# A routed expert stage: where the weight conversions of each expert stand

## The chip, the cores and the metric

One core of one Trainium2 chip runs the whole kernel. The metric is the device time of an execution in microseconds; the kernel before took 772.2 us (median of three runs). TensorE is called PE in the rows, ScalarE ACT, VectorE DVE, GpSimd POOL and SyncE SP.

## What is computed

Three stages follow each other. The first is attention over 4 batches, 8 heads, 512 local and 32 global positions with a band of 32. The second mixes each position with the one before it and runs a feed-forward block with a squared Relu and a gate. The third, which the change is about, sends each of 2176 positions to one of 8 experts:

```
logits = x @ w_gate                       # 8 experts
e      = argmax(logits) or the previous position's e, by a local gate
h      = max(x @ w1[e], 0)                # 512 -> 1024
out    = p[e] * (h @ w2[e])               # 1024 -> 512
```

With this input the experts 0 to 7 get 242, 127, 267, 483, 495, 321, 218 and 23 positions.

## The kernel before, in words

The matmuls work in pairs of parts: each float32 operand is split into a high part (rounded) and a low part (the rest), and `mm3` (L19) issues three matmuls for one product: high by high, high by low, low by high.

The weights of an expert are 4 MB, in 8 pieces of 512 KB: four of w1, then four of w2. A piece is fetched from memory by SP into one of five staging buffers (`st`, `sw`; `part`, L768) and then converted (`split`, L772): ScalarE writes the high part into a slot (L779) and VectorE, or GpSimd for the fourth and the eighth piece (`PP`, L35), subtracts it for the low part (L782). `whole` (L790) does that for the next piece in line, gives its staging buffer back and issues the next fetch (`fetch`, L764). Expert e converts the 8 pieces of expert e+1; the slots are double, one set for even and one for odd experts. Each engine runs its instructions in the order in which the program issues them (`manual_schedule`, L1081), so the place of a `whole()` call in the code is its place in the queues of ScalarE, VectorE, GpSimd and SP.

Experts 0 and 1 have one static tile of 128 rows each (`one`, L941). It calls `tall` (L899): the rows stand still and w1 streams, in two halves of 512 columns. Each half ends in a Relu on ScalarE (L918), then four transposes (`turn`, L902) bring it to the layout of the second product, with a copy on ScalarE (L906) and a subtraction on VectorE (L907). The first half's `turn` comes after two of the four steps of the second half's matmuls; the second half's stands after step 2 of the second product (`TW[2]`, L944). `tall` takes five conversions and places three ahead of the first half, one behind its Relu and one behind the first `turn` (`TW`, L909 to L919). The other three stand after steps 3, 5 and 7 of the second product (L946). Between these stand the preparations of the next expert's rows (`X`): four transposes, a copy on ScalarE and a subtraction on VectorE.

Experts 2 to 6 (`expert`, L961) have a count that is known only at run time (`c`, in units of 32 rows), so their code is a nest of branches. The case with 384 rows or more (`big`) stands first in the code, then 352, 320, 288 and 256 rows (`joined`), then one tile (`single`), then none (`none`). A wide case calls `wide` (L887): w1 stands still and the rows stream in 8 steps of 12 matmuls, each followed by a Relu on ScalarE (L894) and a subtraction on VectorE (L895); there are four PSUM buffers for the steps. Conversions stand behind steps 2, 4 and 6 (`FW`, counted from 0), preparations behind 3, 5 and 7 (`FX`). Then `out_` and `product` do the second product for each tile of rows, 24 matmuls each, and `place` scales the result on VectorE and scatters it from GpSimd.

Of the 8 conversions of an expert, five stand in its side of the branch. The last tile's product (L999) stands behind the join, once for all sides, and holds the other three, after its steps 2, 4 and 6, as well as the preparation of the next expert's third tile (`third`). With the counts above, expert 2 runs the side for 288 rows, 3 and 4 the widest, 5 that for 352 and 6 that for 256. Expert 7 (23 rows) runs `one` again, without conversions.

Of the kernel before, what the change touches and what calls it, by code (L numbers as in the profile page):

```python
# [13 lines left out]
P=128; D=512; F=1024; E=8; SG=32; SL=512; S=544; NB=4; T=2176; HD=64; NK=9; NCH=17  # L14
# [4 lines left out]
def mm3(nc,out,wh,wl,xh,xl,first,last,order=None):  # L19

    i=nc.tensor.matmul(out,wh,xh,start=first,stop=False)  # L21
    if order: order(i)
    nc.tensor.matmul(out,wh,xl,start=False,stop=False)  # L23
    return nc.tensor.matmul(out,wl,xh,start=False,stop=last)  # L24
# [7 lines left out]
GA=6; PA=6  # L32
ND=[k for k,n in enumerate([1, 5, 5, 11, 3, 4, 6, 16]) for _ in range(n)]
V7=[1,1,2,2,3,3,3,3]
PP=(0,0,0,1,0,0,0,1); TW=(1,1,1,(2,4,6),3)  # L35
NR=4; NP=4
FX=(3,5,7); WJ=(288,320,352); MW=352; FW=(2,4,6); NW=(2,3); NST=2
def tiles(n): return 4*n-3
LAT=0.2; DLAT=2.1; SLACK=dict(P=0.15,A=0,D=0,G=0)
def op(e,d,need=(),free=(),when=None): return e,d,need,free,when  # L40
# [1 line left out]
class Sched:  # L42
# [11 lines left out]
    def one(s):  # L54

        for x in sorted(s.L,key=lambda x:(s.t<x[3]+(SLACK.get(x[2][0],0) if x[4] else 0),x[0])):
            e,d,need,free,when=x[2]
            if x[3]>s.t or (e and s.busy[e]>s.t) or any(s.places[k]<need.count(k) for k in need) or (when and not when()): continue
            for k in need: s.places[k]-=1
            if e:  # L60
                end=s.t+d; s.busy[e]=end; later=end+(DLAT if e in "QW" else LAT)
                s.left+=[(later,k) for k in free]
            s.next(x)
            if e: same=x[2] and x[2][0]==e; x[3]=end if same else later; x[4]=not same
            return True
# [686 lines left out]
class Experts:  # L752
# [19 lines left out]
    def split(s,e,which,q,st,pool=False):  # L772
# [4 lines left out]
        else:  # L777
            yield "A",.95
            nc.scalar.activation(h[:,qs],st,AF.Copy)  # L779
        if not pool: pool=PP[4*which+q]  # L780
        yield ("G",2.46) if pool else ("D",1.14)
# [76 lines left out]
    def rows(s,i,n=256): return [t[:,:,i[1]:i[1]+n] for t in s.x[i[0]]]  # L858
# [28 lines left out]
    def wide(s,i,e,N,W=(),X=()):  # L887

        nc=s.nc; W=list(W); X=list(X); w1h,w1l=s.views(e,0); xh,xl=s.rows(i,N); hh,hl=[t[:,:,:N] for t in s.h]
        for f in range(8):  # L890
# [4 lines left out]
            nc.vector.scalar_tensor_tensor(out=hl[:,f],in0=ph,scalar=0.0,in1=hh[:,f].bitcast(F32),op0=ALU.max,op1=ALU.subtract)  # L895
            if f in FX: s.go(X)
            if f in FW: s.go(W)
        s.go(X,8); s.go(W,8)
    def tall(s,i,e,W=(),X=None):  # L899

        nc=s.nc; W=list(W); w1h,w1l=s.views(e,0); xh,xl=s.rows(i); hh,hl=s.h
        def turn(b):  # L902
            pt=s.ps.tile([P,4,P],F32,tag="ph",name="pht2",bufs=4)
            for f in range(4): nc.tensor.transpose(pt[:,f],hs[b][:,f*P:(f+1)*P],s.ident)
            sl=slice(4*b,4*b+4)
            nc.scalar.activation(hh[:,sl,:P],pt,AF.Copy)  # L906
            nc.vector.tensor_sub(hl[:,sl,:P],pt,hh[:,sl,:P].bitcast(F32))  # L907
        hs=[]
        s.go(W,TW[4])  # L909
        for b in range(2):  # L910
            ph=s.ps.tile([P,512],F32,tag="ph",name="pht",bufs=4)
            bs=slice(b*512,(b+1)*512)
            for d in range(4):
                if b and d==2:
                    turn(0); s.go(W,TW[1])
                mm3(nc,ph,xh[:,d,:P],xl[:,d,:P],w1h[:,d,bs],w1l[:,d,bs],d==0,d==3)
            hs.append(s.work.tile([P,512],F32,tag="osb",name="hs",bufs=2))
            nc.scalar.activation(hs[b],ph,AF.Relu)  # L918
            if b==0: s.go(W,TW[0])  # L919
        if X is None: return lambda: turn(1)  # L920
        for f in X: f()
        s.go(W,8); turn(1)
# [18 lines left out]
    def one(s,i,e,b,W,X,o=None):  # L941

        W=list(W); last=s.tall(i,e,[W.pop(0) for _ in range(min(5,len(W)))])
        g=dict((f,[]) for f in range(8)); g[TW[2]].append(last)  # L944
        for f,x in zip((0,3,4),X): g[f].insert(0,x)
        for f,w in zip(TW[3],W): g[f].append(w)  # L946
        s.product(b,e,slice(0,P),g); s.place(b,*s.cols(e,0),o=o)
    def more(s,i,e,k,c,d=0):

# [10 lines left out]
            with two.Else(): single()  # L960
    def expert(s,i,i2,e,c,rows,own,X,third):  # L961

        tc=s.tc; keep=s.loaded,list(s.staged),list(s.free); W=[s.whole]*5
        def begin(k=0,early=True):
            s.loaded,s.staged,s.free=keep[0],list(keep[1]),list(keep[2])
            ch=e*NCH+s.o[e]+2*k
            s.nc.gpsimd.tensor_copy(s.at,s.idx[:,ch:ch+2]); s.nc.gpsimd.tensor_copy(s.by,s.pcol[:,ch:ch+2])
            if early: rows()
        def second(W): s.product(1,e,slice(P,2*P),dict(zip((0,2),([w] for w in W))))
        def big():  # L970
            begin(1,False)
            s.wide(i,e,256,W[:3],[own,lambda: (rows(),X[0]()),X[1]])
            s.out_(0,e,0,slice(0,P),{2:W[:1]}); s.out_(1,e,1,slice(P,2*P),{2:W[:1]})
            with tc.If(c>=tiles(4)) as four:
                s.wide(i2,e,256); second([])
            with four.Else(): s.tall(i2,e,[],[])
        def joined(N):
            begin()
            s.wide(i,e,N,W[:3],X)
            if N>256: s.out_(0,e,2,slice(256,N))  # L980
            second(W[:2])
        def single():
            begin(); s.tall(i,e,W,X)
        def none():
            begin()
            for g in (*W,*X): g()
        L=WJ
        def chain(k):
            if k==len(L): big(); return
            with tc.If(c>=tiles(3)+k+1) as up: chain(k+1)  # L990
            with up.Else(): joined(L[k])
        with tc.If(c>=tiles(2)) as two:
            with tc.If(c>=tiles(3)) as up: chain(0)
            with up.Else(): joined(256)
        with two.Else():
            with tc.If(c>=1) as some: single()
            with some.Else(): none()
        s.place(1,s.by[:,1:2],s.at[:,1:2])
        s.product(0,e,slice(0,P),{1:[third],2:[s.whole],4:[s.whole],6:[s.whole]})  # L999
        s.place(0,s.by[:,0:1],s.at[:,0:1])  # L1000
    def run(s):
        tc=s.tc; K=s.K
# [103 lines left out]
```

## Time and profile before

| | us |
|---|---|
| three runs | 768.14, 772.20, 773.02 |
| median | 772.2 |
| the profiled execution | 773.22 |
| its span, first to last instruction | 771.5 |
| mean granted TensorE clock in it | 0.973 of full speed |

The profiled execution is one more run, with the hardware profiler on; its rows are read below. Its span is 1.7 us shorter than its time, which is what lies before the first and behind the last instruction. The first two stages end near 536 us; expert 0's and 1's tiles run from there to 566, experts 2 to 6 to 754, expert 7 to the end.

### The profile page before, as it was taken

The page shows a single profiled execution, that of the slowest core. Times are in us where ns is not written, and L with a number is a line of the kernel's source. Part 1 is how long each engine was busy: PE and PEld are TensorE (multiplying, and loading weights), DVE is VectorE, ACT ScalarE, POOL GpSimd, SP SyncE. Part 2 cuts the span into 40 slices and gives each one's busy share as a digit, 9 for nine tenths or more (in the row PEclk, how much of TensorE's full clock was granted, in tenths as well). Part 3 has the DMA queues.
Part 4 walks back from the last instruction along what each step waited for, and adds up shares of the span by engine and source line. Part 5 has one row for each costly group of instructions (what it writes and reads, how often), then busy time and mean ns, then how long its engine had stood idle before and what let it go on. Part 6 is the DMA issues. An engine that isn't in the chain of part 4 may idle for free. (4 is left out here: it accounts for less than half of the span.)

```text
span 771.5 us, 13972 instructions
## 1 busy us (share of the span) xinstructions
PE 726.4 (94%) x4702; PEld 611.4 (79%) x4702; DVE 496.9 (64%) x1477; ACT 389.9 (51%) x974; POOL 345.0 (45%) x480
## 2 busy tenths in 40 slices
PE   5888888999999999999999899999989999999997
PEld 3555676889898888898888789777777998889795
DVE  6698878968578587587675693577754624435361
ACT  4787566665265565464664442243643613334251
POOL 5566858644626346437245251211643422404421
PEclk9997799999999999999999999999999999999999
DMA  6585133121210321211110320042884633606530
GB/s 150 134 239 147 58 77 107 42 66 23 65 43 3 79 53 24 73 37 40 42 24 14 123 83 28 19 146 65 314 292 137 240 120 109 205 30 193 165 129 24
DMA packets 93185, 76.37 MB, mean 99 GB/s; under 512 B 70350, under 2 KB 74446, under 8 KB 93074
## 3 DMA queue, kind: packets, MB, share of 16 engines
q1 hardware_dynamic: 89618, 64.27, 28.0%
q0 software_dynamic: 3456, 10.75, 4.1%
q8 instruction: 53, 0.87, 0.5%
q14 instruction: 58, 0.48, 0.2%
HBM read 66.08 MB, written 9.44 MB: 98 GB/s over the span
## 5 line engine op out<-in xcount | busy, mean ns | idle before, releaser
L223 POOL TENSOR_SCALAR pl<-pl,mx 128x192 f32<-128x192 f32 (+1 forms) x128 | 64.0, 512 | 86.1 <-DVE mx L220 40.5
L217 ACT ACTIVATE pl<-pl,mx 128x224 f32<-128x224 f32 (+1 forms) x128 | 58.8, 461 | 34.8 <-DVE mx L214 28.0
L21 PE MATMUL psk<-xs,slot0h 128*128 128x256 f32 x256 | 74.6, 297 | 0.8 <-ACT xs L447 0.8
L23 PE MATMUL psk<-xs,slot0h 128*128 128x256 f32 x256 | 73.6, 289 | 0.0
L24 PE MATMUL psk<-xs,slot0l 128*128 128x256 f32 x256 | 73.4, 288 | 0.0
L449 POOL TENSOR_TENSOR xs<-xm,xs 128x512 fp32r<-128x512 f32 (+1 forms) x36 | 46.7, 1309 | 40.2 <-ACT xs L447 40.2
L894 ACT ACTIVATE hh<-ph 128x256 fp32r<-128x256 f32 (+2 forms) x56 | 22.4, 400 | 76.3 <-PE ph L24 45.9
L442 POOL TENSOR_SCALAR xm<-xT,mut 128x256 f32<-128x256 f32 (+7 forms) x96 | 42.7, 461 | 36.8 <-DVE xT L293 17.9
L21 PE MATMUL psv<-slot1h,kh 128*128 128x512 f32 x136 | 55.3, 406 | 0.0
L23 PE MATMUL psv<-slot1l,kh 128*128 128x512 f32 x136 | 54.3, 400 | 0.0
L24 PE MATMUL psv<-slot1h,kl 128*128 128x512 f32 x136 | 54.2, 398 | 0.0
L895 DVE SCALAR_TENSOR_TENSOR hl<-ph,hh 128x256 fp32r<-128x256 f32 (+2 forms) x56 | 24.7, 442 | 44.2 <-ACT hh L894 42.2
L229 PE MATMUL ptp<-ident,pl 128*128 128x128 f32 x256 | 44.1, 292 | 6.8 <-DVE qT L120 1.3
L21 PEld LDWEIGHTS psk<-xs,slot0h 128*128 128x128 f32 x256 | 48.9, 194 | 1.8 <-ACT xs L447 0.9
L23 PEld LDWEIGHTS psk<-xs,slot0h 128*128 128x128 f32 x256 | 48.9, 191 | 1.2
L24 PEld LDWEIGHTS psk<-xs,slot0l 128*128 128x128 f32 x256 | 48.9, 191 | 0.6
L237 PE MATMUL av<-ph,v 128*128 128x256 f32 x192 | 44.7, 293 | 2.2 <-DVE xT L293 1.8
L866 POOL DMA_INDIRECT xs<-y,idx x23 | 24.8, 1078 | 46.9 <-PE pt L873 22.4
L445 DVE SCALAR_TENSOR_TENSOR xm<-xT,mut,xm 128x256 f32<-128x256 f32 (+7 forms) x96 | 41.4, 464 | 3.2 <-POOL xm L442 3.0
L120 DVE TENSOR_TENSOR plo<-ptp,ph 128x512 fp32r<-128x512 f32 x48 | 32.7, 685 | 14.9 <-ACT ph L118 14.7
L21 PE MATMUL ph<-xh,slot2h 128*128 128x256 f32 (+1 forms) x128 | 37.9, 296 | 4.2 <-issue 4.2
L229 PEld LDWEIGHTS ptp<-ident,pl 128*128 128x128 f32 x256 | 30.6, 148 | 13.8 <-issue 3.3
(740 smaller groups left out, 2396.5 us busy)
## 6 DMA issues: line engine op xcount, KB each, us to landing
st<-in_moe_w_dram SPq DMA_DIRECT2D x42, 512.0 KB
sw<-in_moe_w_dram SPq DMA_DIRECT2D x22, 512.0 KB
y<-r SPq DMA_DIRECT2D x17, 256.0 KB
qn<-in_q_l_dram SPq DMA_DIRECT2D x32, 128.0 KB
kn<-in_k_l_dram SPq DMA_DIRECT2D x32, 128.0 KB
earlyh<-in_moe_w_k_dram SPq DMA_DIRECT2D x8, 512.0 KB
raw<-in_moe_w_v_dram SPq DMA_DIRECT2D x8, 512.0 KB
vn<-in_v_l_dram SPq DMA_DIRECT2D x24, 96.0 KB
```

The source lines that it names most:

```text
L21: i=nc.tensor.matmul(out,wh,xh,start=first,stop=False)
L23: nc.tensor.matmul(out,wh,xl,start=False,stop=False)
L24: return nc.tensor.matmul(out,wl,xh,start=False,stop=last)
L120: nc.vector.tensor_sub(out[1],x,out[0].bitcast(F32))
L217: nc.scalar.activation(p[:,h,ks],p[:,h,ks],AF.Exp,bias=mx[:,h:h+1],scale=-1.0,accum_out=mx[:,4+h:5+h])
L223: nc.gpsimd.tensor_scalar(out=p[:,h,ks],in0=p[:,h,ks],scalar1=mx[:,6+h:7+h],scalar2=0.0,op0=ALU.mult,op1=ALU.add)
L229: nc.tensor.transpose(pt[:,c,h],p[:,h,c*96:c*96+P],s.ident)
L237: nc.tensor.matmul(o,s.v(u,x,i,c),P_[y][:,c],start=c==m==0,stop=c==1 and m==len(parts)-1)
L442: nc.gpsimd.tensor_scalar(out=x[:,u,o:o+k],in0=s.xT[b][:,c,q:q+k],scalar1=m[:,1,c:c+1],scalar2=0.0,op0=ALU.mult,op1=ALU.add)
L445: nc.vector.scalar_tensor_tensor(out=x[:,u,o:o+k],in0=s.xT[b][:,c,1+q:1+q+k],scalar=m[:,0,c:c+1],in1=x[:,u,o:o+k],op0=ALU.mult,op1=ALU.add)
L449: nc.gpsimd.tensor_sub(xl[:,cs,:n],x[:,:,:n],xh[:,cs,:n].bitcast(F32))
L866: s.nc.gpsimd.indirect_dma_start(out=s.xs[i][:,j,:],out_offset=None,in_=s.y,in_offset=IndirectOffsetOnAxis(ap=s.idx[:,ch:ch+1],axis=0))
```

## The change

`TW` becomes a pair: its first entry, for expert 0, holds the old numbers, its second, for the experts from 1 on, puts one conversion ahead of the first half, one behind its Relu, two behind the first `turn` and one behind the second half's Relu. In experts 2 to 6 the three conversions leave the product behind the join; each side of the branch gets eight in its place, with `FW` longer and conversions added to the earlier products.

```diff
-PP=(0,0,0,1,0,0,0,1); TW=(1,1,1,(2,4,6),3)
+PP=(0,0,0,1,0,0,0,1); TW=((3,1,1,0),(1,1,2,1)); TF=(2,4,6)
-FX=(3,5,7); WJ=(288,320,352); MW=352; FW=(2,4,6); NW=(2,3); NST=2
+FX=(3,5,7); WJ=(288,320,352); MW=352; FW=(1,2,4,6,7); NST=2
...
         hs=[]
-        s.go(W,TW[4])
+        n=TW[e>0]
+        s.go(W,n[0])
         for b in range(2):
...
                 if b and d==2:
-                    turn(0); s.go(W,TW[1])
+                    turn(0); s.go(W,n[2])
...
             nc.scalar.activation(hs[b],ph,AF.Relu)
-            if b==0: s.go(W,TW[0])
+            s.go(W,n[1+2*b])
...
-        g=dict((f,[]) for f in range(8)); g[TW[2]].append(last)
+        g=dict((f,[]) for f in range(8)); g[1].append(last)
...
-        for f,w in zip(TW[3],W): g[f].append(w)
+        for f,w in zip(TF,W): g[f].append(w)
...
-        tc=s.tc; keep=s.loaded,list(s.staged),list(s.free); W=[s.whole]*5
+        tc=s.tc; keep=s.loaded,list(s.staged),list(s.free); W=[s.whole]*8
...
-        def second(W): s.product(1,e,slice(P,2*P),dict(zip((0,2),([w] for w in W))))
+        def second(W): s.product(1,e,slice(P,2*P),{0:W[:1],1:W[1:2],2:W[2:]})
...
-            s.out_(0,e,0,slice(0,P),{2:W[:1]}); s.out_(1,e,1,slice(P,2*P),{2:W[:1]})
+            s.out_(0,e,0,slice(0,P),{0:W[:1],2:W[:1],4:W[:1]}); s.out_(1,e,1,slice(P,2*P),{0:W[:1],2:W[:1]})
...
-            s.wide(i,e,N,W[:3],X)
-            if N>256: s.out_(0,e,2,slice(256,N))
-            second(W[:2])
+            s.wide(i,e,N,W[:5 if N==256 else 4],X)
+            if N>256: s.out_(0,e,2,slice(256,N),{0:W[:1],2:W[:1],4:W[:1]})
+            second(W[:3 if N==256 else 1])
...
-        s.product(0,e,slice(0,P),{1:[third],2:[s.whole],4:[s.whole],6:[s.whole]})
+        s.product(0,e,slice(0,P),{1:[third]})
```

The sides `single` and `none` pass `W` on as it is, so they too get eight in place of five.

## Rows read from the trace of the kernel before

**Rows 1.** The page, part 1: busy time, share of the span, instructions.

```profile
PE 726.4 (94%) x4702; PEld 611.4 (79%) x4702; DVE 496.9 (64%) x1477; ACT 389.9 (51%) x974; POOL 345.0 (45%) x480
```

**Rows 2.** Busy time by stretch: expert 1, expert 3 (columns in the first line).

```profile
core 0: us, PE busy (x) PEld busy (x) DVE busy (x) ACT busy (x) POOL busy (x), PEclk, DMA share, GB/s
...
549.90:566.20 16.30, 13.93 (x69) 10.56 (x67) 12.82 (x13) 10.77 (x15) 12.06 (x8) 1.00 0.91 326
...
601.30:648.20 46.90, 46.90 (x305) 42.60 (x305) 19.02 (x31) 16.13 (x28) 14.29 (x13) 1.00 0.40 135
```

**Rows 3.** Waits of TensorE, 535 to 772: us in total, times, longest us.

```profile
PE ph L21 <- issue: 4.5, 3, 2.8
PE pht L904 <- ACT slot2h L779: 1.8, 1, 1.8
PE pht L904 <- ACT hs L918: 0.5, 1, 0.5
```

**Rows 4.** Timeline of ScalarE, expert 1: start us, us, what, [idle before <-releaser].

```profile
549.48 2.22 ACT L779 ACTIVATE slot2h<-sw 128x1024 fp32r<-128x1024 f32 x2
554.38 1.06 ACT L779 ACTIVATE slot2h<-st 128x1024 fp32r<-128x1024 f32 x1 [2.68 <-DMA st<-in_moe_w_dram]
555.34 0.58 ACT L918 ACTIVATE hs<-pht 128x512 f32<-128x512 f32 x1
556.09 1.06 ACT L779 ACTIVATE slot2h<-st 128x1024 fp32r<-128x1024 f32 x1 [0.16 <-DMA st<-in_moe_w_dram]
...
558.98 1.06 ACT L779 ACTIVATE slot0h<-st 128x1024 fp32r<-128x1024 f32 x1 [1.35 <-DMA st<-in_moe_w_dram]
559.95 0.58 ACT L918 ACTIVATE hs<-pht 128x512 f32<-128x512 f32 x1
```

**Rows 5.** Timeline of TensorE, expert 1.

```profile
552.39 0.39 PE L24 MATMUL pht<-slot1h,xl 128*128 128x512 f32 x1
...
555.98 0.65 PE L904 MATMUL pht<-ident,hs 128*128 128x128 f32 x4 [1.84 <-ACT slot2h L779]
...
560.58 0.66 PE L904 MATMUL pht<-ident,hs 128*128 128x128 f32 x4 [0.54 <-ACT hs L918]
...
563.39 0.39 PE L24 MATMUL po<-slot3h,hl 128*128 128x512 f32 x1
```

**Rows 6.** Timeline of VectorE, expert 1.

```profile
560.08 1.23 DVE L782 TENSOR_TENSOR slot0l<-st,slot0h 128x1024 fp32r<-128x1024 f32 x1 [1.72 <-ACT slot0h L779]
561.22 0.68 DVE L876 TENSOR_TENSOR xl<-pt,xh 128x512 fp32r<-128x512 f32 x1
561.90 0.69 DVE L907 TENSOR_TENSOR hl<-pht,hh 128x512 fp32r<-128x512 f32 x1
```

**Rows 7.** Timeline of TensorE: the first matmuls of experts 2, 5 and 6.

```profile
569.08 0.58 PE L21 MATMUL ph<-xh,slot2h 128*128 128x288 f32 x1 [2.77 <-issue]
...
695.74 0.40 PE L21 MATMUL ph<-xh,slot1h 128*128 128x352 f32 x1 [0.35 <-issue]
...
730.77 0.39 PE L21 MATMUL ph<-xh,slot2h 128*128 128x256 f32 x1 [1.41 <-issue]
```

**Rows 8.** Busy time by stretch: ahead of these three, and behind the first.

```profile
564.00:566.20 2.20, 2.20 (x11) 1.56 (x9) 1.74 (x4) 1.81 (x3) 1.87 (x2) 1.00 1.05 420
693.00:695.20 2.20, 2.20 (x11) 1.59 (x9) 2.18 (x2) 1.69 (x2) 0.43 (x1) 1.00 0.11 13
727.00:729.20 2.20, 2.20 (x11) 1.55 (x9) 2.16 (x2) 1.66 (x2) 0.46 (x1) 1.00 0.88 313
...
569.10:572.40 3.30, 3.30 (x14) 3.30 (x15) 0.00 (x0) 0.00 (x0) 2.69 (x6) 0.52 0.89 281
```

**Rows 9.** Timeline of SP's queue, expert 5's end: fetches of weights.

```profile
722.99 2.18 SPq L770 DMA_DIRECT2D sw<-in_moe_w_dram  x2
728.05 3.72 SPq L770 DMA_DIRECT2D st<-in_moe_w_dram  x3
```

**Rows 10.** Timeline of ScalarE, expert 6: the Relu behind step 2.

```profile
735.35 0.39 ACT L894 ACTIVATE hh<-ph 128x256 fp32r<-128x256 f32 x1 [1.03 <-PE ph L24]
```

## The prediction

> **What bounds the kernel now.** I read the page first: TensorE is busy for 94% of the span [rows 1]. A sum over the whole span says little about the part that the diff touches, so I took busy time by stretch next. The reader is to see that in the stretch of expert 3 TensorE is busy for every microsecond, while ScalarE has 16.13 of 46.90, and that only the stretch of expert 1 shows a real hole, 13.93 busy of 16.30 [rows 2]. Then the waits of TensorE alone in the expert stage: three lines carry nearly all of it, 4.5 us in three pieces with no releaser, and 1.8 and 0.5 us behind ScalarE in expert 1 [rows 3]. So the stage is bound by matmuls, and an edit that moves ScalarE, VectorE and GpSimd work can win at most those 6.8 us and what a stall does to the clock. I then looked at each hole by itself.
>
> The two holes of expert 1: the transposes of the first half start at 555.98 after 1.84 us of idle, those of the second half at 560.58 after 0.54 [rows 5]. ScalarE's order explains both. The Relu of the first half starts at 555.34, right behind the third of three conversions, and that one began only at 554.38, when its piece of weights landed; the Relu of the second half (559.95) stands behind the fifth, which began at 558.98, again on a landing [rows 4].
>
> The three pieces without a releaser are the first matmuls of experts 2, 5 and 6 (2.77, 0.35 and 1.41 us) [rows 7]. Those are the experts that leave the nest of branches by an Else; experts 3 and 4, which fall through to the widest case, show no hole. I read them as jumps. In the 2.2 us ahead of them the DMA engines were 1.05, 0.11 and 0.88 busy [rows 8], in the same order as the holes. After the longest hole TensorE's granted clock was 0.52 for the next 3.30 us, its lower level of 1.2 GHz [rows 8]; at full clock that work is 3.30 x 0.52 = 1.7 us, so the hole of expert 2 costs 2.77 + 1.6 = 4.4 us in all.
>
> **The change, part by part.** Number the conversions of an expert 1 to 8. With this input experts 2 to 6 have 267, 483, 495, 321 and 218 rows, so they run the cases 288, widest, widest, 352 and 256. The number of conversions executed stays the same; only their places change.
>
> *Expert 1: the order 3, 1, 1, 0 becomes 1, 1, 2, 1.* Conversion 1 runs at 549.48 as now, about 1.06 us [rows 4]. The first half's last matmul ends at 552.39 + 0.39 = 552.8 [rows 5]; the Relu (0.58) follows at once and ends near 553.4. TensorE has six more matmuls before it needs that, until 554.1, so the 1.84 us hole goes. The transposes end near 554.5, the copy of the first half (0.58) near 555.1, with conversion 2 ahead of it in the gap. Conversions 3 and 4 have data by 554.38 and 556.09 [rows 4]; they run 555.1 to 557.2 and the second Relu to 557.8. TensorE meanwhile does the rest of the second half to about 555.9, and then the first two steps of the product (0.70 each) with four transposes (0.36) between, to about 557.7; up to 0.3 us more if VectorE's low part comes late behind conversion 2. So the second hole nearly goes as well, and the transposes of the second half end near 558.4. Next late is conversion 5. In ScalarE's order it still stands ahead of the second half's copy, and its data land at 558.98 whatever ScalarE did before in expert 1: with five staging buffers it refills the one that expert 0's last conversion gave back. It ends at 560.0, one copy of activations (0.6) follows, and the second half's copy ends at 561.1. On VectorE conversion 5's subtraction (560.08), the activations' (561.22) and then the second half's low part (561.90 for 0.69) keep the times that they have now [rows 6]. Step 4 of the product needs this low part in its third matmul: earliest 562.6, against 563.39 in the trace [rows 5]. What follows is unchanged work, so expert 1 ends 0.8 us earlier: 2.38 us of holes go and 1.6 come back at step 4. Bounds: 2.4 us if conversion 5 lands early enough for everything; the other end is a loss of 0.5, if conversion 2, now 3 us later, lets its staging buffer go late and the refill lands late in turn. I take 0.8, the row of VectorE's low part.
>
> *Experts 2 to 6: conversions out of the last product.* They run beside 24 matmuls that are all back to back (2.20 busy of 2.20 while ScalarE has 1.66) [rows 8], so removing them there frees no time on TensorE by itself. Behind them on VectorE and GpSimd only the last scaling and scatter move up, and nobody on TensorE waits for those.
>
> *The same conversions earlier, after steps 1, 2, 4, 6, 7 of the wide half, and in the earlier products.* In the 256 case ScalarE stands idle for 1.03 us ahead of a Relu [rows 10] and a conversion takes 1.05: it fits to within some hundredths, and four PSUM buffers stand between a late Relu and TensorE. I take 0; without that cover it is under 0.1 us for each added conversion, five experts, so 0.5 us at most. All five staging buffers are full when an expert begins, conversions 6 to 8 need refills that are asked for after 1 to 3, more than 5 us earlier. The fetches that SP issues and GpSimd's two subtractions (conversions 4 and 8) move up with them; in GpSimd's queue conversion 4 still stands behind all gathers that the expert issues, so it delays none of them, and in front of a scatter at most, whose end only GpSimd's next copies wait for.
>
> *Transfers ahead of the jumps.* This is the part that I expect to reach TensorE. SP issues fetches at 722.99 and again at 728.05 [rows 9], because conversions 6 to 8 of expert 5 sit in its last product; they keep the DMA engines at 0.88 just before the jump into expert 6. In the changed kernel the last of them is issued near 723 and lands before 729, so the jump meets quiet DMA engines, like the jump into expert 5 now: 1.41 - 0.35 = 1.06 us less. Bounds: 0 and 1.41. Expert 5's jump has quiet engines already. Expert 2's doesn't change: expert 1 keeps its three conversions in the product, and the fetches behind them still fill the engines.
>
> Sum against the profiled execution: 773.22 - 0.8 - 1.06 = 771.4. That execution lies 1.0 above the median of the runs, 772.2, so as a median I forecast 770.4.
>
> **A rule of the skill that speaks against this.** The Trainium skill, "Runtime: NRT & Kernel Launch", section "Instruction fetch mechanics", says that prefetch is purely sequential and that a taken branch to a target outside of the two fetched pages has to wait for the page. It does not tie the wait to other traffic. By that rule, the trace agrees so far, since only the taken jumps show holes [rows 7]; whether the load or the target's place sets their length, three jumps can't say. By the place alone the sum would be 773.22 - 0.8 = 772.4, which is the first rival.
>
> **The rivals.**
> 1. The jump into expert 6 keeps its hole, since its target stays as far away: only expert 1's 0.8 is left, 771.4 as a median. For it: expert 6's target lies behind more code than expert 5's, whose hole is shorter [rows 7]. Against: expert 2's lies between them and has the longest hole, with the highest load.
> 2. Nothing reaches the end: expert 1's gain is eaten by later landings, the jumps stay: 772.2 (within 0.5). For it: the DMA engines are 0.91 busy over expert 1 [rows 2], so a delay on one piece delays the next.
> 3. More goes than I count: expert 2's jump shrinks too, to 0.35 us, and its slow clock with it: 1.8 + 2.42 + 1.6 = 5.8 us, 766.4. Against: its load should stay.
> 4. Slower: every side of the branch grows by three conversions with their fetches, in seven copies, which moves all jump targets of ScalarE, VectorE, GpSimd and SP, and whatever TensorE's own code gains in semaphore waits moves its targets too. If the jumps into experts 5 and 6 become like expert 2's, with its slow clock, that is (2.77 - 0.35) + (2.77 - 1.41) + 2 x 1.6 = 7.0 us, less 0.8 from expert 1: +6.2, 778.4. It decides where the holes grow as long as expert 2's, which the slow clock followed; the 1.41 us of expert 6 had none behind it. Against: TensorE's instructions hardly change.
>
> **How the numbers follow.** Forecast 0.45, rival 1 0.22, rival 2 0.13, rival 3 0.08, rival 4 0.12. The forecast is the likeliest: 770.4. The three runs of before spread over 768.14 to 773.02, so a median carries some 2 us of its own. From 767.0 to 774.0 the range holds the forecast and rivals 1 and 2 with that spread and the bounds of the two terms (-0.5 to 2.4 and 0 to 1.41); rivals 3 and 4, together 0.20, lie mostly outside. One per cent, about what a measurement of this kernel can tell from no change, is 7.7 us, more than any rival moves the sum; the tails of rivals 3 and 4, with the spread of the runs, give 0.03 for faster and 0.04 for slower, and 0.93 stays within.
>
> **What would show it right or wrong.** Right: in expert 1 the transposes of the first half wait for nothing, a hole of about 1.5 us in all stands ahead of step 4's matmuls, behind ScalarE's copy and VectorE's low part, and conversion 5 still starts on a landing. Expert 6's first matmul has a hole near 0.4 us, with DMA engines nearly idle in the 2 us before; expert 2's keeps some 2.8 us and the slow clock behind it. In the wide halves TensorE has no idle, as now. Wrong: conversion 5 starting well before 558.98 in its expert's time, a hole into expert 6 that keeps 1.4 us over quiet engines, a new wait of TensorE behind a conversion in the first product, or a hole at experts 3 and 4.

## The result, and the profile after

The changed kernel took 779.78 us (median of 20 runs, 773.53 to 782.96) beside 770.99 for the kernel before (20 runs, 765.42 to 775.40): ratio 1.0101, 95% interval [1.0080, 1.0122]. It is slower by about one per cent, 8 us, where 770.4 was forecast and 774.0 was the end of the range. Its profiled execution took 778.59 us, 5.37 more than that of before.

The page of the changed kernel, part 1, answers to [rows 1]. TensorE does the same 4702 matmuls and is busy for about as long; the 5 us are idle time and slow clock.

```profile
span 776.8 us, 13962 instructions
...
PE 728.6 (94%) x4702; PEld 612.7 (79%) x4702; DVE 504.6 (65%) x1477; ACT 389.4 (50%) x974; POOL 341.9 (44%) x480
```

The waits of TensorE from 535 us on, which answer to [rows 3] (us in total, times, longest). Expert 1's two old waits on the transposes are gone. In their place stand two waits at the second product (`hl`, `hh`), and two kinds that the kernel before hasn't got at all: matmuls of a last product (`po`) that wait for nothing visible, and one that waits for a VectorE subtraction of weights (`slot3l`).

```profile
PE ph L21 <- issue: 3.8, 2, 3.6
PE po L21 <- issue: 2.7, 2, 1.4
PE po L21 <- DVE slot3l L782: 2.6, 1, 2.6
PE po L24 <- DVE hl L907: 1.4, 1, 1.4
PE po L21 <- ACT hh L906: 0.6, 1, 0.6
```

The same one by one in TensorE's timeline of the changed kernel; these rows answer to [rows 5] and [rows 7]. The first two belong to expert 1, 569.04 is the first matmul of expert 2, 597.81 the first of expert 2's last product (behind the join of its branches), 698.10 and 733.14 the first of experts 5 and 6, 727.03 and 753.31 the first of the last products of 5 and 6.

```profile
560.24 0.50 PE L21 MATMUL po<-slot3h,hh 128*128 128x512 f32 x1 [0.56 <-ACT hh L906]
562.41 0.50 PE L24 MATMUL po<-slot3h,hl 128*128 128x512 f32 x1 [1.44 <-DVE hl L907]
569.04 0.58 PE L21 MATMUL ph<-xh,slot2h 128*128 128x288 f32 x1 [3.60 <-issue]
...
597.81 0.47 PE L21 MATMUL po<-slot0h,hh 128*128 128x512 f32 x1 [1.37 <-issue]
...
698.10 0.40 PE L21 MATMUL ph<-xh,slot1h 128*128 128x352 f32 x1 [0.15 <-issue]
...
727.03 0.47 PE L21 MATMUL po<-slot3h,hh 128*128 128x512 f32 x1 [1.32 <-issue]
...
733.14 0.28 PE L21 MATMUL ph<-xh,slot2h 128*128 128x256 f32 x1
...
753.31 0.47 PE L21 MATMUL po<-slot0h,hh 128*128 128x512 f32 x1 [2.60 <-DVE slot3l L782]
```

Setting these marks of TensorE's timeline against those of before, both counted from expert 0's first matmul, gives the account:

| stretch | before, us | after, us | difference |
|---|---|---|---|
| expert 0 | 13.11 | 13.26 | +0.15 |
| expert 1, with the jump into expert 2 | 19.20 | 19.77 | +0.57 |
| expert 2, to its last product | 26.27 | 28.78 | +2.51 |
| from there to expert 5's first matmul | 100.38 | 100.28 | -0.10 |
| expert 5, to its last product | 27.45 | 28.94 | +1.49 |
| its last product and the jump into expert 6 | 7.59 | 6.10 | -1.49 |
| expert 6, to its last product | 17.51 | 20.17 | +2.66 |
| from there to the end | 23.22 | 23.47 | +0.25 |
| sum | 234.73 | 240.77 | +6.04 |

The stages ahead, which the change doesn't touch, came out 0.76 us shorter in this execution, hence 5.28 in the span. The windows of the changed kernel, in the columns of [rows 2] and [rows 8], show what lies beside these places. Expert 3 is as full as it was. The stretches at 592.20 and 721.40, on the way out of experts 2 and 5, have the DMA engines at 0.76 and 0.82; those ahead of experts 5 and 6 (695.40, 730.50) at 0.03 and 0.09, where the kernel before had 0.88 ahead of expert 6. Behind the longer hole into expert 2 the clock stays near its lower level of 1.2 GHz (0.50) for 3.30 us and is 0.69 for the next 3.30; in the kernel before it was back at 1.00 by then (the last row, from the kernel before).

```profile
603.90:650.80 46.90, 46.90 (x305) 42.64 (x304) 21.21 (x30) 16.14 (x28) 14.40 (x12) 1.00 0.40 136
...
592.20:597.60 5.40, 4.25 (x19) 3.09 (x17) 0.14 (x1) 0.00 (x0) 3.05 (x2) 1.00 0.76 283
695.40:697.60 2.20, 2.20 (x11) 1.71 (x10) 0.00 (x0) 0.00 (x0) 0.00 (x0) 1.00 0.03 7
721.40:726.80 5.40, 4.32 (x19) 3.16 (x17) 0.00 (x0) 0.00 (x0) 3.21 (x2) 1.00 0.82 273
730.50:732.70 2.20, 2.20 (x12) 1.75 (x11) 0.00 (x0) 0.00 (x0) 0.00 (x0) 1.00 0.09 30
569.06:572.36 3.30, 3.30 (x14) 3.30 (x15) 0.00 (x0) 0.00 (x0) 2.77 (x5) 0.50 0.99 323
572.36:575.66 3.30, 3.30 (x20) 3.30 (x20) 0.77 (x2) 1.17 (x3) 0.00 (x0) 0.69 0.51 183
...
572.40:575.70 3.30, 3.30 (x27) 3.30 (x26) 0.92 (x2) 0.95 (x3) 0.92 (x1) 1.00 0.86 311
```

**First reading: the exits of the branches are jumps too.** TensorE's own sequencer (the part that hands instructions to the engine; `PEldq` in the rows) has rows in the trace, and some of its branches last microseconds. In the kernel before (columns: line, engine, operation, count: shortest, median and longest ns, then the start of the first and last): into expert 2 5.79 us, out of it 3.70, out of expert 5 3.68, into expert 6 5.53.

```profile
L990 PEldq COMPARE_BRANCH  x1: 5790/5790/5790, 563.1 to 563.1; - x1
...
L990 PEldq COMPARE_BRANCH  x1: 3700/3700/3700, 591.2 to 591.2; - x1
...
L990 PEldq COMPARE_BRANCH  x1: 3679/3679/3679, 719.0 to 719.0; - x1
...
L993 PEldq COMPARE_BRANCH  x1: 5532/5532/5532, 725.2 to 725.2; - x1
```

The same four in the changed kernel: the two exits take 5.52 and 5.47, the entry into expert 6 takes 3.64.

```profile
L991 PEldq COMPARE_BRANCH  x1: 5990/5990/5990, 562.9 to 562.9; - x1
...
L991 PEldq COMPARE_BRANCH  x1: 5520/5520/5520, 592.1 to 592.1; - x1
...
L991 PEldq COMPARE_BRANCH  x1: 5474/5474/5474, 721.4 to 721.4; - x1
...
L994 PEldq COMPARE_BRANCH  x1: 3642/3642/3642, 729.1 to 729.1; - x1
```

The long ones are those that meet weight fetches. SP's queue in the changed kernel (answering to [rows 9]) issues the last fetches of experts 2 and 5 at 588.74 to 595.29 and from 718.86 on, around the exits at 592.1 and 721.4:

```profile
588.74 2.60 SPq L770 DMA_DIRECT2D st<-in_moe_w_dram  x3
595.29 0.38 SPq L770 DMA_DIRECT2D sw<-in_moe_w_dram  x1
...
718.86 6.15 SPq L770 DMA_DIRECT2D st<-in_moe_w_dram  x3
```

The sequencer runs some microseconds ahead of the matmuls, and only what a jump takes beyond that lead is seen as a hole. Out of expert 2 the jump starts at 592.12 and the matmuls in hand end at 597.81 - 1.37 = 596.44: the lead is 4.32, and 5.52 - 4.32 and 0.17 to the first matmul make the 1.37. The exit of before, 3.70, fits under such a lead, so it left no trace in [rows 3]. The change moved the burst of fetches from the jump into expert 6 to the jumps out of experts 2 and 5.

**Second reading: the join waits for VectorE.** The hole of 2.60 at 753.31 is of another kind. VectorE's timeline in the changed kernel at expert 6's end, and behind it the durations of the last two subtractions (shortest, median, longest ns):

```profile
746.54 2.12 DVE L782 TENSOR_TENSOR slot3l<-st,slot3h 128x1024 fp32r<-128x1024 f32 x1 [0.52 <-ACT slot3h L779]
748.59 4.58 DVE L782 TENSOR_TENSOR slot3l<-sw,slot3h 128x1024 fp32r<-128x1024 f32 x2
...
L782 DVE TENSOR_TENSOR slot3l<-sw,slot3h x2: 1212/2328/3444, 748.6 to 749.7; 128x1024 fp32r<-128x1024 f32 x2
```

GpSimd's timeline of the same microseconds:

```profile
745.17 2.41 POOL L782 TENSOR_TENSOR slot1l<-st,slot1h 128x1024 fp32r<-128x1024 f32 x1 [7.72 <-ACT slot1h L779]
749.43 2.66 POOL L782 TENSOR_TENSOR slot3l<-st,slot3h 128x1024 fp32r<-128x1024 f32 x1 [1.85 <-ACT slot3h L779]
```

The last subtraction of VectorE starts at 749.73 and takes 3.44 in place of 1.21. GpSimd's ends at 752.09, which leaves 1.08 for VectorE: it seems to have stood still until then. The product behind the join doesn't use `slot3l`, which is expert 7's weight. But its first matmul waits for a count of VectorE's work, and in the changed kernel that count is reached only with this subtraction, which the row of 753.31 names. It belongs to conversion 7; in the kernel before, the subtractions of conversions 6 and 7 stood behind the join (conversion 8's is GpSimd's). It ends at 753.17 and the product starts at 753.31.

### The profile page after: what moved, and what is told of

Its sections match the earlier page's. It is cut to its first block, busy times and chain, and to the rows that moved or that the text cites. A ratio compares the mean times of both kernels' runs of the same rounds, so it can differ in the third digit from the quotient of the medians.

```text
span 776.8 us, 13962 instructions
## 1 busy us (share of the span) xinstructions
PE 728.6 (94%) x4702; PEld 612.7 (79%) x4702; DVE 504.6 (65%) x1477; ACT 389.4 (50%) x974; POOL 341.9 (44%) x480
## 5 line engine op out<-in xcount | busy, mean ns | idle before, releaser
L866 POOL DMA_INDIRECT xs<-y,idx x23 | 27.5, 1194 | 54.5 <-PE pt L873 23.9
```

What stands on the lines that cost most here:

```text
L866: s.nc.gpsimd.indirect_dma_start(out=s.xs[i][:,j,:],out_offset=None,in_=s.y,in_offset=IndirectOffsetOnAxis(ap=s.idx[:,ch:ch+1],axis=0))
```

## The experiments

The theory after the comparison, called A in the expectations: the loss is the two exit jumps lengthened by weight fetches, with the slow clock, and the wait at expert 6's join, while expert 1's new order gains nothing because the jump behind it stays. Rivals: expert 1's new order does it; the jumps are long because code has moved, and not by load; the added conversions slow the wide halves. Ratios are to the kernel before, with 95% intervals.

**1. Expert 1's order alone**, on the kernel before:

```diff
-PP=(0,0,0,1,0,0,0,1); TW=(1,1,1,(2,4,6),3)
+PP=(0,0,0,1,0,0,0,1); TW=((3,1,1,0),(1,1,2,1)); TF=(2,4,6)
...
+        n=TW[e==1]
```

> Only expert 1's order of conversions is changed (1, 1, 2, 1); experts 2 to 6 stay as before. Theory A (a jump of TensorE takes 3.4 to 3.9 us when the DMA engines are quiet and 5.5 to 6 us while weights are fetched, and it hides only as far as its sequencer runs ahead): the product's wait in step 4 holds the sequencer back, so the jump into expert 2 starts no more than 0.3 us earlier, its hole grows from 2.8 to about 3.6 us, and the time stays within 1.5 us of the kernel before. The prediction's step (0.8 us gained, the hole unchanged): 0.8 us faster. Rival B (waits at the join are all of the loss): the same as the prediction's step here, since no join is touched.

Measured: ratio 0.9994 [0.9961, 1.0028]. TensorE's timeline in this kernel: the old holes of expert 1 are gone, but 1.90 stand at step 4 of the product, and the jump, now 6.03 us, leaves a hole of 3.61 where the kernel before had 2.77.

```profile
559.48 0.50 PE L24 MATMUL po<-slot3h,hl 128*128 128x512 f32 x1 [1.90 <-DVE hl L907]
...
566.12 0.58 PE L21 MATMUL ph<-xh,slot2h 128*128 128x288 f32 x1 [3.61 <-issue]
```

From expert 1's first matmul to expert 2's it took 19.75 us, beside 19.20 before and 19.77 in the changed kernel. So the loss of the changed kernel is not expert 1's; a gain of 0.8 us, 0.1%, would lie within the interval, and it is the trace that shows that it did not come.

**2. The sides alone:** the changed kernel with expert 1 in its old order.

```diff
-        n=TW[e>0]
+        n=TW[e>1]
```

> Expert 1 as before; only the sides of experts 2 to 6 are as in the changed kernel. Both theories: the loss is here, 4 to 8 us slower than the kernel before, with holes of about 1.4 us at the last product of experts 2 and 5, 2.6 us at that of expert 6, and less than 0.2 us in front of expert 6; the hole in front of expert 2 is 2.8 us as before.

Measured: 1.0080 [1.0052, 1.0108], so nearly the whole loss is in the sides. Holes of 1.65 and 0.87 out of experts 2 and 5 (jumps 5.80 and 4.96), 2.60 at expert 6's join, none into expert 6 (3.29). The hole into expert 2 was 1.70 (jump 4.73) where 2.8 was expected. The window behind the join's hole shows what the profile of the changed kernel did not: the clock at 0.60, and from the last product of expert 6 to expert 7 7.19 us instead of 5.56.

```profile
751.50:755.50 4.00, 3.85 (x11) 3.04 (x12) 0.76 (x2) 0.00 (x0) 0.99 (x1) 0.60 0.12 46
```

**3. The fetches held in the program:** the changed kernel, where conversions 6 to 8 of a side give their staging buffers back and the next side's first lines issue the fetches, still on SP.

```diff
-        s.fetch()
+        if not s.held: s.fetch()
...
+    def counted(s): s.n8+=1; s.held=s.n8>5; s.whole(); s.held=False
...
-            s.loaded,s.staged,s.free=keep[0],list(keep[1]),list(keep[2])
+            s.loaded,s.staged,s.free=keep[0],list(keep[1]),list(keep[2]); s.n8=0; s.fetch()
```

> The changed kernel, but the fetches that conversions 6 to 8 of experts 2 to 6 would issue wait until the next expert's side begins; the conversions stay where they are. Theory A: the jumps out of experts 2 and 5 fall from 5.5 to under 4 us, their holes of 1.37 and 1.32 us go, the wait of 2.6 us in expert 6 stays, 2.5 to 4 us faster than the changed kernel. Rival B (TensorE waits there for the engines that finish the side's conversions): the conversions haven't moved, so the holes and the time stay.

Measured: 1.0090 [1.0062, 1.0118]; the expected gain did not come. SP has nothing else to wait for: it ran on through the branches and issued the fetches as soon as the staging buffers came free, ahead of TensorE's jump (those at expert 2's end from 588.76 us on; in the changed kernel from 588.74). A later place in the program was no later time. But the miss is a test of its own, since the fetches now also met the jump out of expert 3, which was 3.53 in the kernel before:

```profile
L976 PEldq COMPARE_BRANCH  x2: 64/2848/5632, 623.9 to 641.0; - x2
...
q1 hardware_dynamic: 521, 1.43, 73.3%
```

The first row is that jump, 5.63; the second, from the DMA view of the jump's own stretch, says that weight fetches (the queue `hardware_dynamic`: packets, MB, share of 16 engines) took 73.3%. It left a hole of 1.48 behind expert 3's join, where the kernels before this one had none.

**4. The fetches held by time:** the same, but ScalarE issues the held fetches behind the first Relu of the next expert, so they can't start ahead of the jump.

```diff
+    def release(s):
+        if s.due: s.due=False; s.fetch(s.nc.scalar)
...
             nc.scalar.activation(hh[:,f],ph,AF.Relu)
+            if f==0: s.release()
```

> The changed kernel, but the fetches that follow conversions 6 to 8 of experts 2 to 6 are issued by ScalarE, behind the first Relu of the next expert's wide half, so they can't run before TensorE has begun it. Theory A (load): the jumps out of experts 2 and 5 fall from 5.5 us to under 4.2, their holes of 1.4 and 1.3 us shrink below 0.4, the wait of 2.6 us in expert 6 stays; 2.5 to 4 us faster than the changed kernel. Rival B (the conversions inside the side are waited for): holes and time stay, since no conversion moves.

Measured: 1.0043 [1.0010, 1.0077]. The jumps out of experts 2 and 5 and the weight fetches in the first of them:

```profile
L997 PEldq COMPARE_BRANCH  x1: 3860/3860/3860, 588.7 to 588.7; - x1
...
L997 PEldq COMPARE_BRANCH  x1: 3794/3794/3794, 716.6 to 716.6; - x1
...
q1 hardware_dynamic: 19, 0.05, 3.5%
```

Both holes are gone; the wait of 2.59 at expert 6's join stays. The change to the program is a few lines and moves no conversion, so the jumps go to nearly the same places: load it is, not the place. (Where instructions lie in memory no trace shows.)

**5. Expert 7's subtractions all on VectorE**, on the changed kernel:

```diff
-        if not pool: pool=PP[4*which+q]
+        if not pool: pool=PP[4*which+q] and e<E-1
```

> The changed kernel, but all eight low parts of expert 7's weights are made by VectorE, none by GpSimd. The wait of 2.60 us in front of expert 6's last product is one for VectorE's last subtraction of that side, which took 2.3 us each beside GpSimd's and 1.2 alone. If so: those subtractions take 1.2 us each, the wait falls to under 1 us, 1.5 to 2.5 us faster than the changed kernel. If the wait is for ScalarE or a jump instead: it stays at 2.6.

Measured: 1.0050 [1.0024, 1.0076]. VectorE does two subtractions more in expert 6 and is still done earlier, since none takes over 1.23 us. Conversion 7's, the one that was waited for, ends at 747.24, and TensorE doesn't wait at the join: its product starts at 747.72. (The 2.3 us each of the expectation were the mean of 1.21 and 3.44.)

```profile
743.76 1.22 DVE L782 TENSOR_TENSOR slot3l<-st,slot3h 128x1024 fp32r<-128x1024 f32 x1
744.89 2.35 DVE L782 TENSOR_TENSOR slot3l<-sw,slot3h 128x1024 fp32r<-128x1024 f32 x2
747.17 1.22 DVE L782 TENSOR_TENSOR slot3l<-st,slot3h 128x1024 fp32r<-128x1024 f32 x1
```

So the 2.60 us come from GpSimd's subtractions, which held up the VectorE subtraction that the join waits for. The join does not wait for all of VectorE's side: the last row, conversion 8's, ends at 748.39, after the product has begun. Why the count lies where it does the traces don't show. The holes out of experts 2 and 5 remain (2.12 and 0.80).

**6. Both cures, without expert 1's new order:** 2, 4 and 5 together.

> The changed kernel's sides with all three suspects taken away: expert 1 in its old order, the late fetches issued by ScalarE as above (experts 2 to 6), expert 7's low parts made by VectorE alone. If the jumps' load and VectorE's wait at the join are the whole loss, it lies within 2 us of the kernel before, with no hole over 0.4 us at any join; if conversions inside the side cost anything else, it stays 3 us or more slower.

Measured: 1.0010 [0.9984, 1.0035], the kernel before. No hole is left at any join. Into expert 2 there are still 3.15 us. The causes named are the whole of the loss, as far as the interval shows (some 2 us to either side).

**7. The late fetches in the kernel before**, for the last three conversions of experts 1 to 5, in the hope of shorter jumps into experts 2 and 6:

```diff
-        s.product(0,e,slice(0,P),{1:[third],2:[s.whole],4:[s.whole],6:[s.whole]})
+        s.product(0,e,slice(0,P),{1:[third],2:[s.quiet],4:[s.quiet],6:[s.quiet]})
```

> The kernel before, but the fetches that follow the last three conversions of experts 1 to 5, beside the last product, are issued by ScalarE behind the first Relu of the next expert. Theory A: the jumps into experts 2 and 6 fall from 5.8 and 5.5 us to under 4.2, their holes from 2.8 and 1.4 to under 1.2 and 0.4, the slow clock behind the first goes (1.6 us); 3.5 to 5.5 us faster than the kernel before. If the place of the target sets a jump's length: no difference.

Measured: 1.0013 [0.9986, 1.0040], a miss: 6.11 into expert 2 and 5.72 into expert 6. The DMA view of the jump into expert 2 shows that the fetches of the two conversions before the last three were still under way:

```profile
L996 PEldq COMPARE_BRANCH  x1: 6112/6112/6112, 564.2 to 564.2; - x1
...
q1 hardware_dynamic: 263, 0.92, 42.4%
```

By itself this run speaks against the load as the cause: half the load, and no shorter jump. The last section shows what the two have in common.

**8. The same with expert 1's new order:**

> As the one before, with expert 1's new order of conversions on top. Theory A: the wait in step 4 of expert 1's product holds TensorE's sequencer back, so the jump into expert 2 starts late and little is gained: within 1 us of the kernel without the new order. The prediction's step: 0.8 us faster than that one.

Measured: 1.0035 [1.0009, 1.0060], jumps of 5.97 and 5.22. The order gains nothing here either; it lies 0.2% above run 7, which the intervals don't tell apart.

**9. and 10. Five late fetches in expert 1.** If the two earlier fetches were what kept the jump of run 7 long, they must be held too. Run 9 does it on run 7, run 10 on run 6, which comes first here:

```diff
-[s.whole]*(min(8,16-LN) if e==0 else 5)+[s.quiet]*(3*e)
+[s.whole]*(min(8,16-LN) if e==0 else 3)+[s.quiet]*(5*e)
```

Run 10:

> The changed sides with expert 1 in its old order, expert 7's low parts all on VectorE, the fetches behind conversions 6 to 8 of experts 2 to 6 issued by ScalarE behind the next first Relu (together measured at 1.001 of the kernel before), and now expert 1's fetches behind its conversions 4 to 8 likewise. Only the jump into expert 2 should change. Theory A: from about 5 us or more to 3.3 to 4.2, its hole from 3.15 to under 0.9 and the slow clock behind it gone: 3 to 4 us less, 767 to 769, ratio 0.994 to 0.998. Rival (the target's place): jump and hole stay, ratio 1.001 within 0.3%.

Measured: 0.9960 [0.9933, 0.9987], 768.27 us beside 771.84. The jump into expert 2 takes 3.69 over no weight fetches at all (one packet of that queue); the gathers of rows (`software_dynamic`) do not hold it up. The hole is 1.26 (under 0.9 was expected), in place of 3.15 in run 6, and the clock is 1.00 behind it. (The profile puts this hole down to a conversion on ScalarE, which had ended at 570.30; the jump ended at 570.97.)

```profile
L999 PEldq COMPARE_BRANCH  x1: 3690/3690/3690, 567.3 to 567.3; - x1
...
q0 software_dynamic: 160, 0.52, 46.6%
...
q1 hardware_dynamic: 1, 0.00, 0.0%
...
571.14 0.37 PE L21 MATMUL ph<-xh,slot2h 128*128 128x288 f32 x1 [1.26 <-ACT slot0h L779]
```

Run 9:

> The kernel before; of each of the experts 1 to 6 the conversions 4 to 8 give their staging buffers back without a fetch, and ScalarE issues those five fetches behind the first Relu of the next expert. So no fetch of weights is queued at any jump into an expert (earlier only the last three were held, and the two before them were still in the queue). Theory A (queued weight fetches lengthen the fetch of instructions): the jumps into experts 2 and 6 fall from 5.79 and 5.53 to 3.3 to 4.2 us, the holes from 2.77 and 1.41 to under 0.9 and under 0.3, no slow clock at expert 2's begin; 3 to 5 us less than the kernel before, 766 to 768.5, ratio 0.993 to 0.997, unless the later pieces make ScalarE wait in expert 2. Rival (the length is set by where the target lies in the code): these jumps keep 5 us or more over quiet DMA engines, ratio 1.000 within 0.3%.

Measured: 0.9967 [0.9940, 0.9993], 768.94 us. As it ran, this kernel held five fetches in expert 1 only; the sides of experts 2 to 5 took the first entries of the list, so their fourth and fifth pieces were fetched at once. Accordingly the jump into expert 6 met fetches (45.0%) and took 4.96. That into expert 2 met none and took 4.77, better than 5.79 but longer than theory A said. What held it is open; gathers alone (37.9% here, 46.6% in run 10) don't explain it.

```profile
L997 PEldq COMPARE_BRANCH  x1: 4770/4770/4770, 564.0 to 564.0; - x1
...
q0 software_dynamic: 160, 0.52, 37.9%
```

Both runs are faster than the kernel before by 0.3 to 0.4%, with intervals that just leave out 1; the two can't be told apart.

## Why the prediction was wrong

**What bounds the kernel** was right: TensorE is as full in the wide halves as it was, no wait stands behind an added conversion there, and nearly all that was lost is holes and the clock behind them.

**Expert 1's order** was right in its mechanism and wrong in its worth. Both old holes went, the wait moved to step 4 behind VectorE's low part, conversion 5 still started on a landing, as the prediction had it. The waits at step 4 are 0.56 and 1.44, where 1.6 was forecast. One term was mis-sized there: conversion 5's subtraction took 1.91 us on VectorE instead of the 1.23 of [rows 6], beside a GpSimd subtraction that ended at 560.07. Counted from its first matmul (549.27, before 549.89), expert 1's matmuls end only 0.25 us earlier (565.44 and 566.31). But the step that failed is "what follows is unchanged work". The sequencer waits at step 4 as well, so, counted likewise, it reaches the jump into expert 2 0.38 us later than before (562.89 and 563.13) and with a shorter lead: 565.44 - 562.89 = 2.55 instead of 566.31 - 563.13 = 3.18. The jump itself took 0.20 more. Together the hole grew from 2.77 to 3.60, and the -0.8 became +0.57. Run 1 shows the same in another execution (19.75 us, +0.55).

**"The same conversions earlier: I take 0"** is the step that carried the error. It priced ScalarE's time and the queues of ScalarE and GpSimd, and both prices held. It did not ask where the moved fetches land. The prediction said itself that "the fetches that SP issues ... move up with them", and it knew that loaded DMA engines go with long jumps; but it knew only the three jumps that had left a hole. The exits, 3.70 and 3.68 us long, left none, and stood in no view that it had read: waits show what a jump takes beyond the lead. The sequencer's own rows would have shown every one. Out of expert 2 the new hole cost 1.37; out of expert 5 its hole of 1.32 is nearly all of the 1.49 in the table. Runs 3 and 4 show that it is the load. Of the 2.51 in expert 2's row another 1.0 is not the exit's: the clock behind the jump into expert 2 rose later, and 0.69 over 3.30 us loses 3.30 x 0.31 = 1.0.

**"Removing them there frees no time"** was true of the last product, but the join ahead of it was left out. Conversions 6 to 8 moved from behind the join to ahead of it, where the next matmul waits for a count of VectorE's work that now takes in conversion 7's subtraction. The prediction gave the added subtractions no price on VectorE; this one took 3.44 us beside GpSimd's instead of 1.21. That cost 2.60 us in expert 6, whose side is the shortest, and nothing in the longer ones. Run 5 takes it away.

**The jump into expert 6** was right: quiet DMA engines, and the hole of 1.41 gone altogether where 0.35 was forecast to stay. It is the -1.49 of the table, and expert 5's exit ate it.

**The jump into expert 2** "doesn't change": it kept its load, its 5.8 to 6.0 us and its slow clock; the hole grew for the reason above.

**The target's place.** The Trainium skill, "Runtime: NRT & Kernel Launch", section "Instruction fetch mechanics", says that a taken branch out of the fetched pages stalls for a fetch of the target. The traces agree as far as the fetch goes: each of the 96 branches that lasted 1 us or more holds one 16 KB packet of an instruction queue, and the shortest, over quiet DMA engines, took 3.26 us. The rival drawn from the target's place alone falls, since the same jump out of expert 2 took 5.52 in the changed kernel and 3.86 in run 4.

**The rivals.** Rival 4 had the sign and, with 778.4, the size, by another cause: it let the jumps into experts 5 and 6 grow because targets move. They did not (3.81 and 3.64). The prediction held it unlikely because TensorE's instructions hardly change; but it was the fetches that changed place, and it had followed them only to where they leave. Rivals 1 to 3 all give a time of 772.2 or less, and fall.

In the sum: 773.22 + 0.57 + 2.51 + 1.49 - 1.49 + 2.66 + 0.30 for the rest of the table - 0.76 for the earlier stages = 778.5; the profiled execution took 778.59. The medians stand 8.8 us apart, more than the 5.4 of the two profiles: the profiled execution of before lies 2.2 above its kernel's median of 770.99, that of the changed kernel 1.2 below its own. For the 1.2 the clock behind expert 6's join is a likely reason: from its last product to expert 7 runs 2, 3 and 4, which have the same hole of 2.6, took 7.19, 7.03 and 7.18 us, and the changed kernel's profiled execution 5.65 (before: 5.56), so that it seems to be a lucky one by some 1.5 us. The 2.2 stay open.

## What to carry to other kernels

A transfer that moves away from one jump arrives at another: before moving DMA issues in code with branches, list every taken branch from the sequencer's rows, those without a hole too, and set each beside the DMA load and the lead that hides it. What is moved ahead of a join can come under the counts that another engine waits for there, even where that engine doesn't use the result; so it has to end before that engine arrives, with what a neighbour engine adds to it. And an issue is late only if its engine has something to wait for; a later place in an idle queue changes nothing.

## What the runs showed of the hardware

**Load and jumps.** The twelve traces hold 96 branches of TensorE's sequencer after 530 us that last 1 us or more. I set each beside the share of the weight fetches (`hardware_dynamic`) in its own stretch. With a share of up to 0.09 there are 70: 69 of them took 3.26 to 4.20 us, one 4.77 (run 9). With 0.43 and over there are 25: 24 took 4.73 to 6.39, one 4.05 (run 3, at 0.86). One between, at 0.29, took 4.30. Half the load can cost as much as the whole (6.11 at 0.43, 4.73 at 0.83), and so run 7 missed. As one pair of such rows, the weight fetches in the jump out of expert 2 in the changed kernel, which took 5.52:

```profile
q1 hardware_dynamic: 500, 1.51, 71.4%
...
q8 instruction: 1, 0.02, 1.1%
```

In the kernel before that view has no row of the weight fetches' queue, and the jump took 3.70.

The second row is what the jump waits for, as the DMA packets of the traces show. Each of the 96 branches holds exactly one packet of 16 KB of the instruction queue `q8`, and ends 1.25 to 1.90 us behind it. The packet itself takes about as long with load as without (median 1.02 and 1.06 us). What differs is when it starts: 0.96 us after the branch (median) at a share of up to 0.09, 3.21 at 0.43 and over; out of expert 2 it was 0.87 in the kernel before and 3.13 in the changed one. The rows that stand out follow it too: 1.35 in run 3's 4.05, 2.30 in run 9's 4.77, 3.58 in run 7's 6.11. So beside weight fetches the fetch of the instructions starts late and isn't itself slower; what it waits behind, and why half the load can delay it as much, the traces don't show.

**VectorE beside GpSimd.** Subtractions of 128x1024 that take 1.21 us alone took 2.12 and 3.44 beside GpSimd's, and ended 1.08 us behind these (747.58 to 748.66, 752.09 to 753.17). The Trainium skill, "SBUF — State Buffer", section "SBUF: two separate sides", says that the two engines share a pair of ports as an exclusive lock, so that the later one blocks until the other is done, and doesn't share bandwidth; these numbers agree.

**The clock.** Not every hole is followed by the lower clock: the 2.6 us of idle at expert 6's join were followed by 0.60 over 4 us in run 2 and by 1.00 in the changed kernel's profile; the 3.15 into expert 2 in run 6 were followed by 1.00, the 2.77 in the kernel before by 0.52 [rows 8]. What decides stays open.
